# Spread reads moved to SyncE's queue, product and token sums dealt out over wave slots, two batches' attention set at fixed waves

## The chip, the cores and the metric

The kernel runs on one core of a Trainium2 chip. The metric is the device time of one execution in microseconds: 317.69 us is the median of 8 runs before the change (316.64 to 319.45).

A core has five engines with a queue of their own each: TensorE (PE; its weight loads are shown as PEld), VectorE (DVE), ScalarE (ACT), GpSimd (POOL) and SyncE (SP), which here only issues DMAs. Instructions of one engine run in order; between engines they wait on semaphores.

## What is computed

```python
# attention: B, H, S, D = 4, 4, 1088, 32; S1, S2 are 8 x 32
phi(x) = outer(S1 x, S2 x)                 # 64 features per token
kv = sum_s phi(k)_s v_s^T                  # 64 x 32 per head
z  = sum_s phi(k)_s
attn = (phi(q) kv) / (phi(q) z + 1e-6)
# feed-forward: x is attn as (4352 tokens, 128), d_ff = 1536
gate = sigmoid(x @ w_gate)
out  = (gate * (x @ w_val)) @ w_out        # 4352 x 128
```

The arithmetic is in float32. The weights and S1, S2 arrive as 64-bit floats and are narrowed on the chip in the first 50 us.

## The kernel before

The feed-forward runs over 9 chunks of tokens: eight of 512 (numbers 0 to 7) and one of 256. A chunk is done in waves. A wave is one group of 128 columns of d_ff (two groups in the last chunk): `w1` multiplies the chunk's tokens with w_gate and w_val into one of two PSUM tiles `wave`, ACT takes the sigmoid `sg` (L465), and DVE multiplies it with the value part into `g` (L487, `glu`). A chunk of 512 has 12 waves, so chunk c has waves 12c to 12c + 11.

The second product, with w_out, follows some waves later. Chunks 1 to 7 ("fast") do it in pairs of waves with seven products of half size in place of eight. For this each pair needs sums of its activations, `tsum`, made on POOL by `token_sums` (L325: one difference of 128x512, L328, then two ops of 128x256, L334 and L335), and sums of the weights, `ws` (`weight_sums`, L312, L323). `w2_a` (L388) does four of the products into PSUM bank acc0, three slots after the pair's odd wave; `w2_b` (L416) does three into bank acc1, one slot later. After the sixth pair of a chunk, `w2_a` copies half of its bank on ACT (`other`, L401) and adds up on DVE (`res`, L402 and L405), and `w2_b` does the rest (L428 to L432), transposes the result (L436, 64x1024) and issues the stores. The next chunk's first `w2_a` comes two slots after the last one of this chunk.

The order is written out by hand on TensorE, DVE, ACT and POOL; SP's queue is ordered by the build. `slot(group, waves)` (L510) first records a group of attention work, if there is one, and then for each wave: the waiting `glu`, those second products whose slot has come, and the wave's own matmuls. `moe["n"]` counts waves.

Between the waves stands the attention of batches 1 to 3 (L1181 to L1210). For one batch: `turn_k`, `turn_q` transpose K and Q (DVE); `begin` (L1135) projects them on TensorE (`kps`, `cqps`), copies q's projections out (ACT, `cq`) and calls `spread` (L728). `spread` writes `cq` to DRAM (`dq`, on the queue named `put`), and reads it back in broadcast form: two reads of 576 KB into `qp` and four of 288 KB into `bq` (L738, on the queue named `get`), and eight small ones into `a8` and `b8` (L759, on `put`). Before, `put` is SP and `get` is POOL; for the second half of batch 0 they are ACT and SP. Then `outer` makes the features of K (DVE), `sum_z` sums them, `kv_all` multiplies with V (TensorE), `qmult` makes q's features from `qp` and `bq` (DVE), `weights_z`, `ndt` and `parts` (L1156) do the denominators, numerators and the division into `xT`, the input of later chunks. `load_v` and `load_kq` issue the next batch's loads on SP.

Batch 1 has one wave between its steps (`wn` = 1), batches 2 and 3 have two (`wn` = 2), and the steps follow each other from where the last batch ended, so batch 2 begins at wave 28 or 29 and its `parts` stand near wave 41.

Of the kernel before, what the change touches and what calls it, by code (L numbers as in the profile page):

```python
# [16 lines left out]
P = 128  # L17
# [3 lines left out]
def kernel(  # L21
# [282 lines left out]

    xT = const.tile([P, NTOK], F32, tag="xT")

    moe = {"sum": -1, "ci": 0, "w": 0, "n": 0, "ready": 0, "acc": None, "gate": None, "todo": []}

    def fast(ci):
        return 0 < ci < len(tok_chk) - 1 and tok_chk[ci][1] == TCH  # L310
# [11 lines left out]
        ):  # L322
            nc.gpsimd.tensor_tensor(out=out, in0=in0, in1=in1, op=op)  # L323

    def token_sums(g):  # L325
        t = raw.tile([P, 4, HALF], F32, tag="w_in", name="tsum")
        g1 = g[:, 0].rearrange("p (t x) -> p t x", t=2)
        nc.gpsimd.tensor_tensor(  # L328
            out=t[:, :2],
            in0=g.rearrange("p f (t x) -> p t f x", t=2)[:, 1],  # L330
            in1=g1,
            op=ALU.subtract,
        )
        nc.gpsimd.tensor_tensor(out=t[:, 2], in0=t[:, 1], in1=g1[:, 0], op=ALU.add)  # L334
        nc.gpsimd.tensor_tensor(out=t[:, 3], in0=t[:, 2], in1=g[:, 1, :HALF], op=ALU.subtract)  # L335
        return t

    def product(out, lhsT, rhs, start, stop):
        nc.tensor.matmul(  # L339
# [48 lines left out]
    def w2_a(ci, i, g, t):  # L388
        if i == 0:
            moe["sum"] = ci  # L390
            fst["a"] = pso.tile([P, TCH], F32, tag="acc0", name="prod")
        lo, hi = fst["a"][:64], fst["a"][64:]
        w, first, last = w_sb[:, 2], i == 0, i == NJ // 2 - 1
        product(lo[:, :HALF], w[:, 2 * i, :64], g[:, 0, :HALF], first, last)
        product(hi[:, :HALF], w[:, 2 * i + 1, :64], g[:, 1, :HALF], first, last)
        product(lo[:, HALF:], ws[:, 3, i], g[:, 1, HALF:], False, last)
        product(hi[:, HALF:], ws[:, 1, i], t[:, 2], False, last)
        if last:
            e = fst["e"] = raw.tile([P, 2, 2, HALF], F32, tag="w_in", name="other")[:64]
            r = fst["r"] = raw.tile([P, 5, HALF], F32, tag="w_in", name="res")[:64]  # L400
            nc.scalar.copy(out=e[:, 0], in_=hi.rearrange("p (u x) -> p u x", u=2))  # L401
            nc.vector.tensor_tensor(  # L402
                out=ends(r, 1, 3), in0=twice(lo[:, :HALF]), in1=e[:, 0], op=ALU.add
            )
            nc.vector.tensor_tensor(out=r[:, 2], in0=lo[:, HALF:], in1=r[:, 4], op=ALU.add)  # L405

    def twice(x):
        return bass.AP(tensor=x.tensor, offset=x.offset, ap=[list(x.ap[0]), [0, 2], [1, HALF]])
# [7 lines left out]
    def w2_b(ci, i, g, t):  # L416
# [9 lines left out]
        if last:  # L426
            e, r = fst["e"], fst["r"]
            nc.scalar.copy(out=e[:, 1], in_=hi.rearrange("p (u x) -> p u x", u=2))  # L428
            nc.vector.tensor_tensor(out=r[:, 0], in0=lo[:, HALF:], in1=e[:, 1, 1], op=ALU.add)
            nc.vector.tensor_tensor(out=r[:, 4], in0=r[:, 4], in1=r[:, 0], op=ALU.add)  # L430
            nc.vector.tensor_tensor(out=r[:, 3], in0=r[:, 4], in1=e[:, 1, 0], op=ALU.subtract)
            nc.vector.tensor_tensor(  # L432
                out=ends(r, 2, 2), in0=twice(lo[:, :HALF]), in1=ends(r, 2, 2), op=ALU.add
            )
            o_sb = sbA.tile([P, 2, TCH // 32, 32], F32, tag="o_sb", name="o_sb")
            nc.vector.transpose(  # L436
                out=o_sb[:64].rearrange("p d t x -> p (d t x)"),
                in_=r[:, 1:].rearrange("p u x -> p (u x)"),
            )
            store(ci, lambda g4: o_sb[32 * (g4 % 2) : 32 * (g4 % 2) + 32, g4 // 2])  # L440

    def w1():

# [41 lines left out]
        def glu():  # L485
# [3 lines left out]
            if not fast(ci):  # L489
                lag = 3 if ci else 2  # L490
                part = (ci, j0, jn, g.rearrange("p (j t) -> p j t", j=jn))
                todo.append((n + lag, lambda: w2(*part)))
            elif odd:
                part = (ci, j0 // 2, pair, token_sums(pair))
                todo.append((n + 3, lambda: w2_a(*part)))
                todo.append((n + 4, lambda: w2_b(*part)))

# [12 lines left out]
    def slot(group, waves):  # L510
# [4 lines left out]
        for _ in range(waves):  # L515
            more = moe["ci"] < len(tok_chk)
            if more and sum(tok_chk[moe["ci"]]) > moe["ready"]:
                break
            glu()
            while todo and todo[0][0] <= moe["n"]:  # L520
                todo.pop(0)[1]()
            if more:
# [612 lines left out]
    def begin(b):  # L1135
        glu()
        kps(b)
        cq[b] = qcomp(b, (0, 1), (psm, "wave"))
        spread(b, (0, 1), cq[b], nc.sync, nc.gpsimd)

    def q01():
        spread(0, (1,), qcomp(0, (1,), (ps2, "two")), nc.scalar, nc.sync)
# [24 lines left out]
    def kv_all(b):  # L1167
        kv(b, ZS[b])
        kvd(b)
# [8 lines left out]
    slot(lambda: part01(lambda: narrow_w(NJ - 1, 3)), 1)  # L1178
    slot(last01, 1)
    v_t[1] = load_v(1)  # L1180
    for b in range(1, B):  # L1181
        more = b + 1 < B
        wn = 1 if b == 1 else 2
        turn_k(b)
        if b > 1:
            turn_q(b, 0)
        slot(None, wn)
        if b == 1:
            turn_q(b, 0)
        turn_q(b, 1)  # L1190
        slot(lambda: begin(b), 1)
        for pi in range(2):
            outer(b, pi)
            slot(None, wn)
        for step in range(2):
            sum_z(b, step)
            slot(None, wn)
            if b == 1 and step == 0:
                masks()
        slot(lambda: kv_all(b), wn)  # L1200
        if more:
            v_t[b + 1] = load_v(b + 1)
        qmult(b, 0)
        weights_z(b)
        slot(lambda: ndt(b), 1)
        qmult(b, 1)
        load_kq(b + 1)
        if b == 1:
            slot(None, 1)
        slot(lambda: parts(b), wn + 5)  # L1210
    slot(None, 10**3)


# [28 lines left out]
```

## Time and profile before

| | |
|---|---|
| median of 8 runs | 317.69 us |
| the profiled execution | 316.64 us, span on the core 314.8 us |
| TensorE, DVE, POOL, ACT busy | 294.7, 184.3, 160.2, 88.9 us |
| `g` (DVE L487) | x102, mean 683 ns |
| token sums on POOL (L328, L334, L335) | x42 each, mean 1376, 729, 816 ns |
| spread reads on POOL (L738) | x18, mean 590 ns to issue; 8.2 us (`qp`) and 9.9 us (`bq`) median to landing |
| granted TensorE clock, mean | 0.989 |

The span goes from the first instruction to the last. A line of a timeline gives the start in us from the start of the span, the duration, the engine, the source line, what is written and read, the shape, and in brackets how long the engine had been idle before it and what ended that. The end of a wave's matmuls is best seen from the start of its sigmoid, 0.04 to 0.1 us later.

### The profile page before, as it was taken

What the parts mean: (1) busy time and instruction counts of PE and PEld (TensorE: products, weight loads), DVE (VectorE), ACT (ScalarE), POOL (GpSimd) and SP (SyncE); (2) the same over time, 40 slices, a digit from 0 to 9 for tenths busy, and PEclk for the clock granted to TensorE, in tenths of its full rate; (3) what the DMA queues carried; (4) which work ended last, traced back from release to release, by engine and by line L of the source; (5) the groups of instructions that cost most, each with busy time, mean ns of one, the idle gap of its engine ahead of it and who ended that gap; (6) DMA issues with size and microseconds to landing.
All of it is one profiled execution on the core that took longest, in us unless ns stands there. A gap on an engine that the chain in (4) does not pass through costs nothing.

```text
span 314.8 us, 5511 instructions
## 1 busy us (share of the span) xinstructions
PE 294.7 (94%) x2176; PEld 152.6 (48%) x2176; DVE 184.3 (59%) x310; ACT 88.9 (28%) x164; POOL 160.2 (51%) x196
## 2 busy tenths in 40 slices
PE   8899999489999779988999999899999999999995
PEld 3444432135455344543564455443556465546853
DVE  6997798807737735388247853894327323722461
ACT  3566523102123212330224221222223222322320
POOL 1556560964363495515657874436463654566300
PEclk9999999959999999999999999999999999999999
DMA  7994241872400387126001880002000200010021
GB/s 221 354 315 111 66 143 52 188 172 77 144 0 0 73 186 157 31 47 173 3 0 49 192 171 3 2 1 35 1 0 2 33 0 2 7 29 0 0 35 17
DMA packets 30553, 24.35 MB, mean 77 GB/s; under 512 B 20480, under 2 KB 25728, under 8 KB 30528
## 3 DMA queue, kind: packets, MB, share of 16 engines
q1 hardware_dynamic: 27024, 16.15, 19.3%
q0 software_dynamic: 2592, 7.08, 9.9%
q10 hardware_dynamic: 912, 0.77, 0.9%
q8 instruction: 17, 0.28, 0.4%
q14 instruction: 8, 0.07, 0.1%
HBM read 20.73 MB, written 3.26 MB: 76 GB/s over the span
## 4 chain that ended last, share of the span: by engine, by line
PE 62%; DVE 12%; POOL 10%; DMA 8%; issue 5%; ACT 1%; SPq 1%; POOLq 0%; DVEq 0%
PE wave L457 40%; PE prod L339 17%; POOL head L118 3%; DMA v<-in_v_dram 3%; POOL tsum L328 2%; DMA w_in<-in_moe_w_out_dram 2%; PE moeout L370 2%; POOL ws L323 2%; DVE g L487 2%; DMA w_in<-in_moe_w_gate_dram 1%; DVE o_sb L436 1%; POOL bq L738 1%; DVE head L109 1%; DVE w_sb L127 1%; PE kvz L788 1%
## 5 line engine op out<-in xcount | busy, mean ns | idle before, releaser
L457 PE MATMUL wave<-xT,w_sb 128*64 128x512 f32 (+3 forms) x820 | 213.6, 572 | 0.8 <-DVE g L487 0.8
L487 DVE TENSOR_TENSOR g<-wave,sg 128x512 f32<-128x512 f32 x102 | 69.6, 683 | 110.0 <-ACT sg L465 105.7
L457 PEld LDWEIGHTS wave<-xT,w_sb 128*64 128x64 f32 (+1 forms) x820 | 82.5, 141 | 69.4 <-issue 50.6
L465 ACT ACTIVATE sg<-wave 128x512 f32<-128x512 f32 x102 | 61.0, 598 | 193.4 <-PE wave L457 186.1
L328 POOL TENSOR_TENSOR tsum<-g 128x512 f32<-128x512 f32 x42 | 57.8, 1376 | 95.5 <-DVE g L487 95.5
L339 PE MATMUL prod<-tsum,ws 128*64 128x256 f32 x252 | 68.0, 387 | 7.4 <-POOL tsum L334 7.4
L339 PEld LDWEIGHTS prod<-tsum,ws 128*64 128x64 f32 x252 | 33.2, 139 | 21.7 <-POOL tsum L334 8.8
L335 POOL TENSOR_TENSOR tsum<-tsum,g 128x256 f32<-128x256 f32 x42 | 34.3, 816 | 3.3
L339 PE MATMUL prod<-g,w_sb 128*64 128x256 f32 x168 | 34.0, 382 | 0.1
L334 POOL TENSOR_TENSOR tsum<-tsum,g 128x256 f32<-128x256 f32 x42 | 30.6, 729 | 3.3
L339 PE MATMUL prod<-tsum,w_sb 128*64 128x256 f32 x84 | 25.6, 388 | 0.0
L339 PE MATMUL prod<-g,ws 128*64 128x256 f32 x84 | 25.0, 379 | 0.0
L339 PEld LDWEIGHTS prod<-g,w_sb 128*64 128x64 f32 x168 | 15.9, 137 | 18.1 <-issue 16.8
L118 POOL TENSOR_TENSOR head<-head,tail 128x384 int32<-128x384 int32 (+2 forms) x14 | 13.3, 952 | 18.2 <-DVE head L109 15.1
L370 PE MATMUL moeout<-g,w_sb 128*128 128x512 f32 (+1 forms) x48 | 18.9, 503 | 0.3 <-DVE w_sb L127 0.3
L339 PEld LDWEIGHTS prod<-tsum,w_sb 128*64 128x64 f32 x84 | 11.3, 139 | 7.9 <-issue 6.9
L339 PEld LDWEIGHTS prod<-g,ws 128*64 128x64 f32 x84 | 11.5, 137 | 3.3
L370 PEld LDWEIGHTS moeout<-g,w_sb 128*128 128x128 f32 x48 | 8.5, 189 | 8.3 <-issue 4.2
L646 DVE TENSOR_TENSOR kp<-kab 128x1152 f32<-128x1152 f32 (+2 forms) x10 | 10.6, 1081 | 0.0
L766 DVE TENSOR_TENSOR qp<-qp,bq 128x1152 f32<-128x1152 f32 (+1 forms) x7 | 9.1, 1296 | 0.0
L738 POOL DMA_DIRECT2D qp<-dq x6 | 3.6, 595 | 10.3 <-DMA dq<-cq 10.3
L436 DVE STREAM_TRANSPOSE o_sb<-res 64x1024 f32<-64x1024 f32 x7 | 8.7, 1236 | 0.2
(114 smaller groups left out, 196.1 us busy)
## 6 DMA issues: line engine op xcount, KB each, us to landing
qp<-dq POOLq DMA_DIRECT2D x6, 576.0 KB, 8.2
bq<-dq POOLq DMA_DIRECT2D x12, 288.0 KB, 9.9
v<-in_v_dram SPq DMA_DIRECT2D x16, 144.0 KB, 4.2
kq<-in_k_dram SPq DMA_DIRECT2D x3, 544.0 KB, 3.8
kq<-in_q_dram SPq DMA_DIRECT2D x3, 544.0 KB, 4.7
w_in<-in_moe_w_out_dram SPq DMA_DIRECT2D x6, 256.0 KB, 7.2
w_in<-in_moe_w_gate_dram SPq DMA_DIRECT2D x5, 256.0 KB, 5.5
w_in<-in_moe_w_val_dram SPq DMA_DIRECT2D x5, 256.0 KB, 6.7
```

Of the source, the lines that this page charges most:

```text
L118: nc.gpsimd.tensor_tensor(out=head, in0=head, in1=tail, op=ALU.add)
L328: nc.gpsimd.tensor_tensor(out=t[:, :2], in0=g.rearrange("p f (t x) -> p t f x", t=2)[:, 1], in1=g1, op=ALU.subtract,)
L334: nc.gpsimd.tensor_tensor(out=t[:, 2], in0=t[:, 1], in1=g1[:, 0], op=ALU.add)
L335: nc.gpsimd.tensor_tensor(out=t[:, 3], in0=t[:, 2], in1=g[:, 1, :HALF], op=ALU.subtract)
L339: nc.tensor.matmul(out=out, lhsT=lhsT, rhs=rhs, start=start, stop=stop, skip_group_check=True)
L370: nc.tensor.matmul(out=moe["acc"][:, :tw], lhsT=w_sb[:, 2, j, :], rhs=g[:, jj, :tw], start=(j == 0), stop=(j == NJ - 1),)
L436: nc.vector.transpose(out=o_sb[:64].rearrange("p d t x -> p (d t x)"), in_=r[:, 1:].rearrange("p u x -> p (u x)"),)
L457: nc.tensor.matmul(out=wv[d, which, jj * tw + o : jj * tw + o + tp], lhsT=w_sb[:, which, j0 + jj, d], rhs=xT[:, t0 + o : t0 + o + tp], sta ...
L465: nc.scalar.activation(out=sg, in_=wv[:, 0], func=ACTF.Sigmoid)
L487: nc.vector.tensor_tensor(out=g, in0=wv[:, 1], in1=sg, op=MUL)
L646: eng.tensor_tensor(out=KP[b][:, pi, j0:j1].rearrange("p j m (i l) -> p (j m) i l", i=R), in0=bass.AP(tensor=a0.tensor, offset=a0.offset, ...
L766: nc.vector.tensor_tensor(out=q0, in0=q0, in1=half(BQ[b], n), op=MUL)
```

## The change

Four things are edited.

1. In `begin`, the spread reads (`get`) go on SP's queue instead of POOL's.
2. `token_sums` makes its four sums as four POOL ops of 128x256 instead of one of 128x512 and two of 128x256: the first after the even wave's `g`, three after the odd wave's.
3. The sums of a chunk's products become small functions in a list `moe["late"]`, of which `slot` runs one per wave, after `glu`. Only the first (and the two ACT copies) stays in `w2_a` and `w2_b`. The transpose becomes two of 64x512. The stores come with the second one.
4. Batches 2 and 3 no longer follow with two waves between steps: each step is recorded when the wave count has reached a number of a table. Batch 1 keeps its order, written out.

```diff
-    def token_sums(g):
-        t = raw.tile([P, 4, HALF], F32, tag="w_in", name="tsum")
-        g1 = g[:, 0].rearrange("p (t x) -> p t x", t=2)
-        nc.gpsimd.tensor_tensor(
-            out=t[:, :2],
-            in0=g.rearrange("p f (t x) -> p t f x", t=2)[:, 1],
-            in1=g1,
-            op=ALU.subtract,
-        )
-        nc.gpsimd.tensor_tensor(out=t[:, 2], in0=t[:, 1], in1=g1[:, 0], op=ALU.add)
-        nc.gpsimd.tensor_tensor(out=t[:, 3], in0=t[:, 2], in1=g[:, 1, :HALF], op=ALU.subtract)
-        return t
+    def token_sums(g, t, odd):
+        def sub(u, in0, in1):
+            nc.gpsimd.tensor_tensor(out=t[:, u], in0=in0, in1=in1, op=ALU.subtract)
+
+        if not odd:
+            sub(0, g[:, 0, HALF:], g[:, 0, :HALF])
+            return
+        sub(2, g[:, 1, HALF:], t[:, 0])
+        sub(3, t[:, 2], g[:, 1, :HALF])
+        sub(1, g[:, 1, HALF:], g[:, 0, HALF:])
...
             nc.scalar.copy(out=e[:, 0], in_=hi.rearrange("p (u x) -> p u x", u=2))
-            nc.vector.tensor_tensor(
-                out=ends(r, 1, 3), in0=twice(lo[:, :HALF]), in1=e[:, 0], op=ALU.add
-            )
-            nc.vector.tensor_tensor(out=r[:, 2], in0=lo[:, HALF:], in1=r[:, 4], op=ALU.add)
+
+            add(ends(r, 1, 3), twice(lo[:, :HALF]), e[:, 0])
+            moe["late"] += [lambda: add(r[:, 2], lo[:, HALF:], r[:, 4])]
+
+    def add(out, in0, in1, op=ALU.add):
+        nc.vector.tensor_tensor(out=out, in0=in0, in1=in1, op=op)
...
             nc.scalar.copy(out=e[:, 1], in_=hi.rearrange("p (u x) -> p u x", u=2))
-            nc.vector.tensor_tensor(out=r[:, 0], in0=lo[:, HALF:], in1=e[:, 1, 1], op=ALU.add)
-            nc.vector.tensor_tensor(out=r[:, 4], in0=r[:, 4], in1=r[:, 0], op=ALU.add)
-            nc.vector.tensor_tensor(out=r[:, 3], in0=r[:, 4], in1=e[:, 1, 0], op=ALU.subtract)
-            nc.vector.tensor_tensor(
-                out=ends(r, 2, 2), in0=twice(lo[:, :HALF]), in1=ends(r, 2, 2), op=ALU.add
-            )
             o_sb = sbA.tile([P, 2, TCH // 32, 32], F32, tag="o_sb", name="o_sb")
-            nc.vector.transpose(
-                out=o_sb[:64].rearrange("p d t x -> p (d t x)"),
-                in_=r[:, 1:].rearrange("p u x -> p (u x)"),
-            )
-            store(ci, lambda g4: o_sb[32 * (g4 % 2) : 32 * (g4 % 2) + 32, g4 // 2])
+
+            def fifth_seventh():
+                add(ends(r, 2, 3), twice(lo[:, :HALF]), ends(r, 2, 2))
+                add(r[:, 0], lo[:, HALF:], e[:, 1, 1])
+
+            def last_sums():
+                add(r[:, 3], r[:, 4], e[:, 1, 0], op=ALU.subtract)
+                add(r[:, 3:5], ends(r, 3, 2), twice(r[:, 0]))
+
+            def turned(d):
+                nc.vector.transpose(
+                    out=o_sb[:64, d].rearrange("p t x -> p (t x)"),
+                    in_=r[:, 1 + 2 * d : 3 + 2 * d].rearrange("p u x -> p (u x)"),
+                )
+
+            def turn_store():
+                turned(1)
+                store(ci, lambda g4: o_sb[32 * (g4 % 2) : 32 * (g4 % 2) + 32, g4 // 2])
+
+            moe["late"] += [fifth_seventh, last_sums, lambda: turned(0), turn_store]
...
-            elif odd:
-                part = (ci, j0 // 2, pair, token_sums(pair))
+                return
+            if not odd:
+                moe["t"] = raw.tile([P, 4, HALF], F32, tag="w_in", name="tsum")
+            token_sums(pair, moe["t"], odd)
+            if odd:
+                part = (ci, j0 // 2, pair, moe["t"])
...
             glu()
+            if moe["late"]:
+                moe["late"].pop(0)()
             while todo and todo[0][0] <= moe["n"]:
...
-        spread(b, (0, 1), cq[b], nc.sync, nc.gpsimd)
+        spread(b, (0, 1), cq[b], nc.sync, nc.sync)
...
+    def until(n):
+        slot(None, n - moe["n"])
+
+    plan = {2: (27, 29, 30, 31, 32, 34, 36, 37, 38, 39, 42, 44)}
+    plan[3] = (48, 49, 51, 53, 56, 57, 58, 59, 60, 61, 63, 68)
+    for b in range(2, B):
+        at = iter(plan[b])
+        until(next(at))
         turn_k(b)
-        if b > 1:
-            turn_q(b, 0)
...
+        for n in range(2):
+            until(next(at))
+            turn_q(b, n)
+        until(next(at))
         slot(lambda: begin(b), 1)
         for pi in range(2):
+            until(next(at))
             outer(b, pi)
-            slot(None, wn)
         for step in range(2):
+            until(next(at))
             sum_z(b, step)
-            slot(None, wn)
...
-        slot(lambda: kv_all(b), wn)
-        if more:
+        until(next(at))
+        slot(lambda: kv_all(b), 1)
+        if b + 1 < B:
             v_t[b + 1] = load_v(b + 1)
+        until(next(at))
         qmult(b, 0)
+        slot(lambda: ndt(b), 1)
         weights_z(b)
-        slot(lambda: ndt(b), 1)
+        until(next(at))
         qmult(b, 1)
         load_kq(b + 1)
...
-        slot(lambda: parts(b), wn + 5)
+        until(next(at))
+        slot(lambda: parts(b), 1)
     slot(None, 10**3)
```

In the built order, each chunk's late sums stand as follows, if s is the slot of its last `w2_a`: the sum r[2] in slot s + 1 (before the last `w2_b`), `fifth_seventh` in s + 2, `last_sums` in s + 3, the first transpose in s + 4, the second and the stores in s + 5. Chunk 7 has s = 98, and the last wave is 101.

## The prediction

> **What bounds the kernel now.** I read the page first, then the waits, then the timeline engine by engine around the waits that end on TensorE. From the page:
>
> ```profile
> span 314.8 us, 5511 instructions
> PE 294.7 (94%) x2176; PEld 152.6 (48%) x2176; DVE 184.3 (59%) x310; ACT 88.9 (28%) x164; POOL 160.2 (51%) x196
> PEclk9999999959999999999999999999999999999999
> PE 62%; DVE 12%; POOL 10%; DMA 8%; issue 5%; ACT 1%; SPq 1%; POOLq 0%; DVEq 0%
> ```
>
> TensorE is the bound: no other engine passes 59%. What can be won is the time in which it has nothing, or runs at half clock (the 5 in the ninth slice, near 63 to 70 us). The timeline of TensorE, 40 to 130 us:
>
> ```profile
> 64.04 0.69 PE L339 MATMUL prod<-tsum,ws 128*64 128x256 f32 x1 [5.32 <-POOL tsum L334]
> 64.95 3.62 PE L457 MATMUL wave<-xT,w_sb 128*64 128x512 f32 x7
> ...
> 105.28 0.72 PE L713 MATMUL cqps<-qT,skq 64*32 64x288 f32 x16 [1.69 <-DVE qT L547]
> ...
> 115.99 0.43 PE L339 MATMUL prod<-tsum,ws 128*64 128x256 f32 x1 [1.68 <-POOL tsum L334]
> ```
>
> It waits 5.32 us for a token sum of POOL; the wave after that takes 3.6 us instead of about 1.9. Why POOL is late stands in its own timeline, 44 to 65 us:
>
> ```profile
> 46.43 0.59 POOL L323 TENSOR_TENSOR ws<-w_sb 128x192 f32<-128x192 f32 x1
> 55.28 0.76 POOL L738 DMA_DIRECT2D qp<-dq  x1 [8.26 <-DMA dq<-cq]
> ...
> 58.72 0.68 POOL L323 TENSOR_TENSOR ws<-w_sb 128x192 f32<-128x192 f32 x1
> ...
> 61.75 1.44 POOL L328 TENSOR_TENSOR tsum<-g 128x512 f32<-128x512 f32 x1
> 63.27 0.72 POOL L334 TENSOR_TENSOR tsum<-tsum,g 128x256 f32<-128x256 f32 x1
> ```
>
> POOL stood 8.26 us in front of the first spread read of batch 1 until q's features had landed in DRAM, issued six reads (3.5 us), and only then made the weight sums and token sums queued behind. Around batch 2 the Vector engine is late (its timeline, 95 to 106 us):
>
> ```profile
> 98.19 1.29 DVE L536 STREAM_TRANSPOSE kT<-kq 128x1088 f32<-128x1088 f32 x1
> ...
> 102.64 1.24 DVE L436 STREAM_TRANSPOSE o_sb<-res 64x1024 f32<-64x1024 f32 x1
> 103.81 0.64 DVE L487 TENSOR_TENSOR g<-wave,sg 128x512 f32<-128x512 f32 x1
> 104.38 0.75 DVE L547 STREAM_TRANSPOSE qT<-kq 128x576 f32<-128x576 f32 x1
> ```
>
> From 97.1 us it has no gap: chunk 1's sums, K's and q's transposes stand in one heap, and cqps waits for the last one. The starts of the sigmoid (ACT L465) are the beat of the waves:
>
> ```profile
> 57.92 0.60 ACT L465 ACTIVATE sg<-wave 128x512 f32<-128x512 f32 x1 [1.12 <-PE wave L457]
> ...
> 71.25 0.60 ACT L465 ACTIVATE sg<-wave 128x512 f32<-128x512 f32 x1 [2.03 <-PE wave L457]
> ...
> 219.32 0.60 ACT L465 ACTIVATE sg<-wave 128x512 f32<-128x512 f32 x1 [1.99 <-PE wave L457]
> ...
> 229.26 0.60 ACT L465 ACTIVATE sg<-wave 128x512 f32<-128x512 f32 x1 [2.00 <-PE wave L457]
> ```
>
> Four quiet slots (waves 66 to 70) take 9.94 us, so 2.485 each; from wave 65 (216.73) to 98 (298.67) it is 81.94/33 = 2.483. The last 98 us are at TensorE's own pace; nothing is to be won there.
>
> **What the Trainium skill says.** "TensorE: Matmul & The Clock Gate", Part 1: after an idle window of about 3.4 us the array's clock is halved until it has been busy as long. The trace agrees: 5.32 us idle, then a granted clock of 0.50 from 64.0 to 69.4 us. "SBUF — State Buffer", section on the two separate sides: a Vector op with both inputs in SBUF and a GpSimd op that reads SBUF exclude each other for a whole instruction. It agrees: POOL's L335 at 180.32 took 1.80 us instead of 0.72 beside the Vector engine's L822. "DMA: Bandwidth & Descriptors", "Issuing engines are not separate DMA queues": changing the issuer saves only the issuer's time. The b = 0 reads, already on SP, land like POOL's (4.9 us for qp, against 5.3 to 6.4 for the first of each POOL batch).
>
> **The change part by part.** Losses first, each a stretch between sigmoid starts less the same stretch undisturbed.
> - Waves 15 to 17, 13.33 us less 4.97: 8.36 (5.32 idle, and 5.4 us at half clock costs 2.7).
> - Waves 28 to 29, 5.77 less 3.87 (the same step of batch 3, 49 to 50): 1.90.
> - Waves 29 to 33, 11.79 less 9.94: 1.85.
> - Waves 37 to 41 (kv, ndt, parts of batch 2), 17.20 less 14.47 (waves 17 to 21, the same for batch 1): 2.73.
> - Waves 50 to 54, 11.38 less 9.94: 1.44. Waves 58 to 62, 15.20 less 14.47: 0.73. Waves 62 to 65, 8.87 less 7.46: 1.41.
>
> Sum 18.42 us. All stretches between keep the beat.
>
> Reads to SP: 6 issues of 0.6 us and the wait leave POOL for each of three batches. POOL then meets wave 12's g at 51.7: one difference 0.7, four weight sums 2.6, wave 13's g at 55.8, and t[2] stands near 56.6; the product that waited until 64.0 can run at 58.3. The first loss and those after 29 and 50 lose their cause. What SP queues behind: the reads wait there for dq as POOL did (SP's a/b reads already stood at 55.0), issue until about 59, and the eight a/b reads follow. In the built order the last six of these each wait for the landing of the DMA eight places before, a spread read. Spread traffic took from 56.7 to 69.6 us; SP's b = 0 half took about the same per byte, so qp/bq land near 63 and 70, the last b8 near 72. With the stall gone waves 16 to 20 end near 60.4, 62.8, 66.9, 69.8, 72.4. qmult(1,0) comes after wave 17's g at 64.2, so it is free; qmult(1,1) after 69.2 waits up to 1 us, covered because g has about 3.2 us from its wave's end until the wave after next needs its bank, and takes 1.4; denj at 72.4 is a tie: 0 to 1 us, I take 0.3.
>
> Token sums: 1.38 + 0.73 + 0.82 = 2.9 us in one burst become one 0.7 after the even g and three (2.2 to 2.3) after the odd one. TensorE's first need, t[2], is ready 0.75 us after the odd g instead of 2.1. No cost: POOL stays near 3.0 of 4.97 us a pair.
>
> Product sums: 0.68 + 4 x 0.42 + 0.68 + 1.24 = 4.3 us of the Vector engine in two slots become 0.68, 0.42, 1.1, 1.1, 0.65, 0.65 in six. A slot leaves it 2.485 - 0.68 = 1.8 us, so each fits. What is late next is the bank: the last read of acc1 (fifth_seventh) ends about 0.64 + 0.69 + 1.1 + small gaps = 2.5 us after its wave's end, the next product into that bank comes after 0.86 + 1.72 = 2.58. A tie, at seven chunk ends; from 0 to 0.7 each, if a POOL op is in the way. I take 0.5 in all.
>
> Fixed waves: batch 2 begins at wave 31 instead of 28, parts at 44 and 68. Per slot the attention adds at most 1.3 (kT), 0.75 (qT), 0.95 (kab), 1.35 (outer), 2.3 (second step of sum_z), 1.2 or 1.4 (qmult); the worst sums in one slot (turn_k with the sum r[2], 1.7; last_sums with qmult, 2.5 at wave 42) pass 1.8 by less than g's spare 1.8. parts has no chunk sums beside it (these end at slots 43 and 67), as in batch 1, where it cost nothing. Reads have from wave 31 to 39 and 53 to 61, 20 us for about 16 (stores that stand before dq on SP included). So I count the other five losses as gone.
>
> End: chunk 7's two transposes now stand behind the last g (before: 302.1), and its four stores on SP in front of the final pair. They issue from about 311.0 for 1.8 us, where the final pair went at 311.5 and 311.9 with 1.7 us to land: +1.3 us.
>
> Sum: 314.8 - 18.4 + 0.3 + 0.5 + 1.3 = 298.5. Around the span lie 316.64 - 314.8 = 1.84, giving 300.3; the profiled execution was the fastest of eight, 1.05 under the median 317.69. Forecast 301.3, own range 299.5 to 303.5.
>
> **The rivals.**
> - Vector stalls only move. The heaps are dealt out but the work stays (59% busy), and lock waits of up to 0.7 us come on each two-input op. Then only POOL's losses go, 8.36 + 1.85 + 1.44 = 11.65: 316.64 - 11.65 + 2.1 + 1.05 = 308.1. Against it: the slots worked out above.
> - The bank: if each of seven chunk ends costs 0.65 more, 4.5 us: 305.8. For it the tie; against it that waves 75 and 87 now show a delayed g and no loss.
> - Slower: SP serves the reads late. dq, stores, six reads and eight short ones now go in one line. If a batch's reads took twice as long, 29 us from dq's landing, qmult(1,0) would hold g from 67.4 (64.2 + 3.2) to near 84, TensorE would stand 16 us and then run at half clock (3 us), and batches 2 and 3 would lose about 10 each: 301.3 + 39 = 340. It decides only above some 13 us for the first half; SP's own b = 0 reads needed under 8 from issue.
> - The change doesn't do what it says: the built order has each step at its wave, so hardly.
>
> **How the numbers follow.** Forecast 0.72, moved stalls 0.13, bank 0.10, slower 0.04, nothing 0.01. So faster by over 0.3% (1 us, what this kernel's runs can tell) 0.95, within 0.01, slower 0.04. The range goes from 298.5, below nearly all of the forecast's, to 306.5, which takes in the bank and leaves out the rest of moved stalls and the slow case, under 2 in 10.
>
> **What would show it.** No POOL issue of reads; the PEclk row without a 5; wave 17's sigmoid near 62.9; no wait of TensorE above 0.5 us after 58; 4 slots per 9.94 us past wave 20 but for kps/cqps, kv and parts; the last store issued some 1.3 us after the last transpose. A wait of cqps, nps or a wave for DVE over 1 us would speak for the first rival, of prod for DVE res at slots 28, 29, 40, 41 and so on for the second, of DVE qp for a DMA for the third.

## The result and the profile after

The changed kernel takes 300.58 us (median of 11 runs, 299.95 to 303.55), the kernel before 317.69 us (32 runs); the ratio is 0.947, its 95% interval 0.945 to 0.949. The forecast was 301.3. The profiled execution's span is 298.9 us, and the working had come to 298.5.

The page of the changed kernel, with the rows that answer to those shown of before:

```profile
span 298.9 us, 5583 instructions
PE 290.0 (97%) x2176; PEld 152.5 (51%) x2176; DVE 187.5 (63%) x317; ACT 88.9 (30%) x164; POOL 160.9 (54%) x220
PEclk9999999999999999999999999999999999999999
PE 77%; DMA 13%; DVE 4%; POOL 2%; SPq 2%; issue 1%; ACT 1%; POOLq 0%; DVEq 0%
```

TensorE's busy time fell by under 5 us (294.7 to 290.0; matmuls at half clock are part of that), the rest of the 15.9 us was its idle time: its busy share of the span rose from 94 to 97%, its share of the chain that ended last from 62 to 77%. VectorE and GpSimd fell from 12 and 10% of that chain to 4 and 2% without having less to do: 187.5 us and 160.9 us are no less than before. DMA rose from 8 to 13%: between 52 and 73 us the chain now goes through batch 1's write of `dq` and the reads of it on SP. The 5 in the clock row is gone.

The waits of TensorE in the changed kernel (what waits, for what; us in total, times, longest), the two of them that lie after 20 us:

```profile
PE moeout L368 <- DVE res L405: 1.4, 1, 1.4
...
PE denj L932 <- DMA b<-dq: 0.3, 1, 0.3
```

The wait for token sums, 7.4 us in three pieces before, does not occur, nor do those for qT and qp. What is left is one wait of 1.4 us that the prediction did not have, and one of 0.3 for a late read. The same in the beat of the waves (timeline of ScalarE; first column the start):

```profile
57.82 0.60 ACT L474 ACTIVATE sg<-wave 128x512 f32<-128x512 f32 x1 [1.12 <-PE wave L466]
60.40 0.60 ACT L474 ACTIVATE sg<-wave 128x512 f32<-128x512 f32 x1 [1.97 <-PE wave L466]
62.97 0.60 ACT L474 ACTIVATE sg<-wave 128x512 f32<-128x512 f32 x1 [1.97 <-PE wave L466]
...
280.86 0.60 ACT L474 ACTIVATE sg<-wave 128x512 f32<-128x512 f32 x1 [1.12 <-PE wave L466]
```

These are waves 15, 16, 17 and 98. From 15 to 17 it takes 5.15 us where it took 13.34, and from 15 to 98 223.04 where it took 240.75: 17.71 us gained. The last stretches give some back: from 98 to 101 the wave starts take 10.76 instead of 9.61, and from wave 101 to the end it is 7.32 instead of 6.55. The start is 0.1 shorter. -17.71 + 1.15 + 0.77 - 0.1 = -15.9, which is the difference of the spans, 314.8 - 298.9.

The heap that VectorE had around the start of batch 2 is spread out. In its timeline the sums (`res`), the transposes of K and q and the halves of `o_sb` now stand in different slots, each with a `g` between them, and TensorE's `cqps` (last line, from TensorE's timeline) no longer waits for `qT`:

```profile
90.42 1.29 DVE L551 STREAM_TRANSPOSE kT<-kq 128x1088 f32<-128x1088 f32 x1
91.65 0.65 DVE L496 TENSOR_TENSOR g<-wave,sg 128x512 f32<-128x512 f32 x1
...
98.46 0.76 DVE L562 STREAM_TRANSPOSE qT<-kq 128x576 f32<-128x576 f32 x1
99.15 0.64 DVE L496 TENSOR_TENSOR g<-wave,sg 128x512 f32<-128x512 f32 x1
99.73 0.68 DVE L440 STREAM_TRANSPOSE o_sb<-res 64x512 f32<-64x512 f32 x1
...
101.25 0.69 PE L728 MATMUL cqps<-qT,skq 64*32 64x288 f32 x16
```

### The profile page after: what moved, and what is told of

It is laid out like the page before. It is cut to its first block, busy times and chain, and to the rows that moved or that the text cites. A ratio compares the mean times of both kernels' runs of the same rounds, so it can differ in the third digit from the quotient of the medians.

```text
span 298.9 us, 5583 instructions
## 1 busy us (share of the span) xinstructions
PE 290.0 (97%) x2176; PEld 152.5 (51%) x2176; DVE 187.5 (63%) x317; ACT 88.9 (30%) x164; POOL 160.9 (54%) x220
## 4 chain that ended last, share of the span: by engine, by line
PE 77%; DMA 13%; DVE 4%; POOL 2%; SPq 2%; issue 1%; ACT 1%; POOLq 0%; DVEq 0%
PE wave L466 49%; PE prod L337 20%; DMA bq<-dq 5%; PE moeout L368 3%; DMA w_in<-in_moe_w_out_dram 2%; POOL head L118 2%; DMA kq<-in_q_dram 2%; DMA w_in<-in_moe_w_val_dram 2%; PE nps L997 1%; DMA v<-in_v_dram 1%; DVE w_sb L127 1%; SPq L753 1%; DVE head L109 1%; PE kvz L803 1%; DMA dq<-cq 1%
## 5 line engine op out<-in xcount | busy, mean ns | idle before, releaser
L466 PE MATMUL wave<-xT,w_sb 128*64 128x512 f32 (+3 forms) x820 | 211.1, 566 | 0.0
L466 PEld LDWEIGHTS wave<-xT,w_sb 128*64 128x64 f32 (+1 forms) x820 | 84.2, 140 | 65.7 <-issue 49.4
L327 POOL TENSOR_TENSOR tsum<-g 128x256 f32<-128x256 f32 x84 | 66.8, 798 | 24.6 <-DVE g L496 24.4
L327 POOL TENSOR_TENSOR tsum<-g,tsum 128x256 f32<-128x256 f32 x42 | 34.2, 814 | 65.3 <-DVE g L496 65.1
L337 PE MATMUL prod<-tsum,ws 128*64 128x256 f32 x252 | 62.3, 381 | 0.0
L337 PEld LDWEIGHTS prod<-tsum,ws 128*64 128x64 f32 x252 | 30.9, 136 | 16.7 <-issue 12.6
L327 POOL TENSOR_TENSOR tsum<-tsum,g 128x256 f32<-128x256 f32 x42 | 33.6, 800 | 3.3
L337 PE MATMUL prod<-g,w_sb 128*64 128x256 f32 x168 | 34.8, 382 | 0.0
L337 PEld LDWEIGHTS prod<-g,w_sb 128*64 128x64 f32 x168 | 15.9, 136 | 19.1 <-issue 15.7
L440 DVE STREAM_TRANSPOSE o_sb<-res 64x512 f32<-64x512 f32 x14 | 9.6, 688 | 0.0
L405 DVE TENSOR_TENSOR res<-prod,other 64x512 f32<-64x512 f32 (+1 forms) x14 | 7.6, 544 | 3.1 <-ACT other L399 3.1
```

What stands on the lines that cost most here:

```text
L327: nc.gpsimd.tensor_tensor(out=t[:, u], in0=in0, in1=in1, op=ALU.subtract)
L337: nc.tensor.matmul(out=out, lhsT=lhsT, rhs=rhs, start=start, stop=stop, skip_group_check=True)
L405: nc.vector.tensor_tensor(out=out, in0=in0, in1=in1, op=op)
L440: nc.vector.transpose(out=o_sb[:64, d].rearrange("p t x -> p (t x)"), in_=r[:, 1 + 2 * d : 3 + 2 * d].rearrange("p u x -> p (u x)"),)
L466: nc.tensor.matmul(out=wv[d, which, jj * tw + o : jj * tw + o + tp], lhsT=w_sb[:, which, j0 + jj, d], rhs=xT[:, t0 + o : t0 + o + tp], sta ...
```

## The experiments

The runs stand in groups; those of one group ran beside the same runs of the kernel before. All stretches below are differences of sigmoid starts in one profiled execution each, in us (the last digit can be off by one from the rounded starts); the first two columns are the two kernels of the change. The kernel before was slower beside some groups than beside others, so medians of different groups are compared by their ratios to it; its own median is in the last row.

| waves | before | changed | reads on SP only | reads back | old order | sums at once | token sums back | best (chunk 7 at once, batch 1 later) |
|---|---|---|---|---|---|---|---|---|
| 15-17 | 13.34 | 5.14 | 6.56 | 10.95 | 5.14 | 5.14 | 6.56 | 5.14 |
| 20-22 | 7.42 | 8.39 | 7.42 | 7.42 | 11.20 | 9.20 | 7.42 | 7.46 |
| 22-28 | 14.67 | 14.67 | 14.67 | 14.67 | 17.07 | 14.67 | 14.67 | 15.06 |
| 28-68 | 121.48 | 110.60 | 120.96 | 113.03 | 111.10 | 112.55 | 111.98 | 110.60 |
| 98-101 | 9.61 | 10.76 | 9.62 | 10.76 | 10.76 | 9.59 | 10.76 | 9.30 |
| 101-end | 6.55 | 7.32 | 6.35 | 7.38 | 7.33 | 6.36 | 7.33 | 6.36 |
| span | 314.8 | 298.9 | 307.0 | 306.4 | 304.6 | 300.1 | 301.1 | 296.2 |
| median | 317.69 | 300.58 | 308.92 | 308.42 | 305.55 | 301.43 | 302.72 | 297.66 |
| kernel before, same group | 317.69 | 317.69 | 319.06 | 319.06 | 319.06 | 319.06 | 317.96 | 317.96 |

### The reads alone

```
-        spread(b, (0, 1), cq[b], nc.sync, nc.gpsimd)
+        spread(b, (0, 1), cq[b], nc.sync, nc.sync)
```

> The kernel before with one part of the change alone: all reads of the spread buffer issued on SP. Theory (each part removes its own losses): of the 18.4 us of loss in the table of waves, waves 15 to 17 (8.36), 29 to 33 (1.85) and 50 to 54 (1.44) belong to reads on POOL, so about 11.6 us go, less the costs of batch 1's later landings (about 1): span 303 to 305, and no half clock. Rival (the order of the attention and of the sums is what matters, the reads' queue is secondary): the stalls of waves 15 to 17 only change hands, span 311 or more. If a/b reads on SP land later than need in batch 1, a wait of about 1 us appears in waves 19 to 21.

Measured: 308.92 us, ratio 0.969 (0.965 to 0.974), span 307.0. Profile against profile that is 7.8 us gained where the theory had some 11 and the rival under 4: it lies between. By the medians of the group (319.06 for the kernel before, of three runs) it is 10.1, because all three of those runs were slower than the profiled one. The theory's span of 303 to 305 was missed either way, and so was its "no half clock". Waves 15 to 17 give 6.78 us of the 8.36, waves 29 to 33 1.91 as expected, waves 50 to 54 nothing (11.37 before and here). The rest of the first stretch is still a token sum, in the timeline of TensorE of this run:

```profile
59.59 0.43 PE L339 MATMUL prod<-tsum,ws 128*64 128x256 f32 x1 [1.19 <-POOL tsum L334]
```

And 1.42 us were lost in waves 37 to 41, where the change touches nothing: the clock fell there (see the last section).

### The reads put back on POOL in the changed kernel

The same line, the other way round.

> The changed kernel with one part undone: 12 of the spread reads of batches 1 to 3 go back to POOL's queue. Theory: POOL issues reads ahead of wave 14's pair's ws and token sums again, TensorE waits over 4 us near 58 to 65 us and runs at half clock after it: 7 to 9 us back there, 0 to 1.5 in each of batches 2 and 3, less the 1 us of batch 1's late landings; span 305.5 to 309.5. Rival (the token sums split in two, with one operation ahead of the odd half, or the fixed waves, already took the stall away): span within 2 of the changed kernel's 298.9.

Measured: 308.42 us, 0.968 (0.963 to 0.972), span 306.4, 7.5 longer than the changed kernel's: the theory's range, and not the rival's. (The reads that went back are 18, six in each of three batches; the 12 of the expectation is a slip.) Waves 15 to 17 lose 5.81 again, less than the 7 to 9 that were expected there, 33 to 37 1.43, 54 to 58 0.85; batch 1's waves 20 to 22 win 0.97 back. GpSimd's timeline in this run:

```profile
51.88 0.73 POOL L327 TENSOR_TENSOR tsum<-g 128x256 f32<-128x256 f32 x1 [4.80 <-DVE g L496]
54.82 0.76 POOL L753 DMA_DIRECT2D qp<-dq  x1 [2.21 <-DMA dq<-cq]
...
57.17 1.15 POOL L753 DMA_DIRECT2D bq<-dq  x2
58.26 1.08 POOL L323 TENSOR_TENSOR ws<-w_sb 128x192 f32<-128x192 f32 x1
...
61.72 0.90 POOL L327 TENSOR_TENSOR tsum<-g,tsum 128x256 f32<-128x256 f32 x1
```

The even half's difference runs at 51.88, ahead of the reads, and then all else stands behind them until 58.3, as in the kernel before; TensorE waits 3.88 us where it waited 5.32 in the kernel before (the theory had over 4). In the changed kernel nothing stands between:

```profile
51.71 0.73 POOL L327 TENSOR_TENSOR tsum<-g 128x256 f32<-128x256 f32 x1 [4.79 <-DVE g L496]
52.40 0.59 POOL L323 TENSOR_TENSOR ws<-w_sb 128x192 f32<-128x192 f32 x1
53.07 0.59 POOL L323 TENSOR_TENSOR ws<-ws,w_sb 128x192 f32<-128x192 f32 x1
53.74 1.59 POOL L323 TENSOR_TENSOR ws<-w_sb,ws 128x192 f32<-128x192 f32 x1
...
55.84 1.85 POOL L327 TENSOR_TENSOR tsum<-g,tsum 128x256 f32<-128x256 f32 x1
```

### The old order of batches 2 and 3

```
-    plan = {2: (27, 29, 30, 31, 32, 34, 36, 37, 38, 39, 42, 44)}
-    plan[3] = (48, 49, 51, 53, 56, 57, 58, 59, 60, 61, 63, 68)
+    wn = 2
     for b in range(2, B):
...
-            until(next(at))
-            outer(b, pi)
+            outer(b, pi)
+            slot(None, wn)
```

> The changed kernel with the attention of batches 2 and 3 in its old order of two waves a step, the sums still dealt out and the reads on SP. Theory: some of the stalls behind VectorE in waves 28 to 33, 37 to 41 and 54 to 65 come back, since heaps of attention meet the dealt sums: 2 to 5 us, span 301 to 304. Rival (the dealt sums alone had taken these stalls away, fixed waves only move work): within 1 us of 298.9. Second rival (dealt sums need the fixed waves, else a bank is held): 305 or more, with the wait of TensorE at product sums behind ScalarE or VectorE.

Of the six slots that stood between batch 1's last step and batch 2 in the kernel before only one is left in it, so batch 2 begins five waves earlier: K's and q's feature matmuls of batch 2 come after wave 23 and not after wave 28. Measured: 305.55 us, 0.959 (0.951 to 0.966), span 304.6, 0.6 above the theory's range. Waves 28 to 68, which it was about, take only 0.5 us more, but some 1.3 us of batch 2's matmuls have moved out of that stretch; over waves 22 to 68, which hold batches 2 and 3 in both kernels, it is 2.9 (128.17 against 125.28). The largest loss is in waves 20 to 25 (5.2 us, of which these moved matmuls are 1.3), where batch 1's own reads were late in this execution (timeline of TensorE):

```profile
73.88 0.49 PE L932 MATMUL denj<-b,zw 64*64 64x160 f32 x4 [1.38 <-DMA b<-dq]
74.67 0.49 PE L932 MATMUL denj<-b,zw 64*64 64x160 f32 x4 [0.31 <-DMA b<-dq]
```

and half clock came after it, from 76.0 to 79.4 us. The program up to that point is the changed kernel's own. So this run could not tell what it was made for; it was repeated below without the late reads.

### The product sums at once

```
-            moe["late"] += [lambda: add(r[:, 2], lo[:, HALF:], r[:, 4])]
+            add(r[:, 2], lo[:, HALF:], r[:, 4])
...
-            moe["late"] += [fifth_seventh, last_sums, lambda: turned(0), turn_store]
+            fifth_seventh()
+            last_sums()
+            turned(0)
+            turn_store()
```

> The changed kernel with the product sums of a chunk run where its products end, as before, instead of dealt out over later slots; reads on SP and fixed waves stay. Theory: VectorE has five to six sums and two transposes in a row at each of eight chunk ends, so g of the next wave is late where attention sits in the same slots: 1.5 to 4 us in waves 28 to 65, less the 0.5 us of the bank tie, the 1.1 us before chunk 8 and up to 0.8 at the tail: span 298 to 301. Rival (the dealt sums are what the schedule rests on): 303 or more. Rival (they are worth nothing, the fixed waves do it all): 296 to 297.5.

Measured: 301.43 us, 0.946 (0.940 to 0.952), span 300.1: the theory. Waves 28 to 68 lose 1.95, with g late for two waves (0.43 and 0.50 us of TensorE's time, after 131 and 197 us); chunk 8 and the tail win back 1.17 + 0.96, a late read of batch 1 costs 0.8, and in this execution the waves start 0.7 later. So, in this version of the kernel, dealing out wins 1.95 us beside the attention and gives 2.13 back at the end: by the time alone this part of the change is worth next to nothing.

### The changed kernel again

> The changed kernel itself, beside the next three on the same chip: median 300.3 to 301.5 us, profiled span 298.5 to 300. A second profile also tells how much of the wait in batch 1 (waves 20 to 22 took 8.39 us against 7.42 before) changes from run to run: the two kernels profiled since, whose program is the same up to there, took 9.20 and 11.20.

Measured: 300.28 us, 0.945 (0.943 to 0.947), span 298.5. In this execution waves 20 to 22 take 7.42 us and no wait for b is left. So batch 1's loss comes and goes with the landing of its reads: 8.39, 7.42, 9.20, 11.20, and 7.60 in the run after the next, all with the same program up to there. SP's last read of batch 1 was issued at 71.76, 70.32, 73.35, 72.95 and 71.14 us. Counted from the sigmoid of wave 15 that is 13.9, 12.1, 14.8, 15.2 and 13.2 us: the later the read, the larger the loss.

### The token sums in one burst

```
-            token_sums(pair, moe["t"], odd)
             if odd:
-                part = (ci, j0 // 2, pair, moe["t"])
+                part = (ci, j0 // 2, pair, token_sums(pair))
```

> The changed kernel with the token sums as before: three GpSimd operations after the odd half's g (the first 128x512) instead of one after the even half's g and three short ones after the odd's. The prediction counted the split at nothing of its own: span within 0.5 of the changed kernel. Rival, from the run with the reads alone, where TensorE still waited 1.19 us for a token sum at 59.6: the split is what takes that rest away, so waves 15 to 17 take 6.5 us instead of 5.14 and the span is 1.2 to 1.6 us longer.

Measured: 302.72 us, 0.953 (0.951 to 0.955), against 300.28 of the changed kernel in the same group: 2.4 us, more than the rival had. Waves 15 to 17 take 6.56, as with the reads alone, so the 1.42 us left over there are this burst, and the prediction's "no cost" for the change of the token sums was in truth a gain that it left out; and waves 28 to 68 lose another 1.38 in pieces of 0.1 to 0.5. GpSimd's timeline:

```profile
55.96 2.32 POOL L328 TENSOR_TENSOR tsum<-g 128x512 f32<-128x512 f32 x1 [6.42 <-DVE g L498]
58.36 1.58 POOL L334 TENSOR_TENSOR tsum<-tsum,g 128x256 f32<-128x256 f32 x1
60.02 0.73 POOL L335 TENSOR_TENSOR tsum<-tsum,g 128x256 f32<-128x256 f32 x1
```

It stood idle for 6.42 us before the burst, and the second operation of the burst, whose result the product needs, ended at 59.9. In the changed kernel this sum, t[2], was ready at 57.7, because its first operand had been made at 51.7.

### The last fast chunk at once

```
-            moe["late"] += [fifth_seventh, last_sums, lambda: turned(0), turn_store]
+            rest = [fifth_seventh, last_sums, lambda: turned(0), turn_store]
+            if ci == len(tok_chk) - 2:
+                for f in rest:
+                    f()
+            else:
+                moe["late"] += rest
```

and the same for r[2] in w2_a.

> The changed kernel with the sums of the last fast chunk alone (chunk 7) run where its products end; chunks 0 to 6 stay dealt out. Theory: the wait of 1.42 us before chunk 8's first moeout goes (waves 98 to 101 take 9.6 us instead of 10.76), the tail from wave 101's sigmoid to the end gives back up to 0.77: span 1.1 to 1.9 us shorter than the changed kernel's. Rival: with the sums in a heap, g of wave 99 or 100 comes late and the same time is lost there: within 0.4.

Measured: 298.77 us, 0.940 (0.938 to 0.943), 1.5 under the changed kernel's 300.28; span 295.8. Waves 98 to 101 take 9.30 instead of 10.76, and the tail 6.34 instead of 7.32. The theory's mechanism holds, and nothing is lost in their place. By the median the gain lies in its range of 1.1 to 1.9; the profiled execution, the fastest of the six, gained 2.7 against the second profile of the changed kernel, since both stretches gave more than expected (1.46 and 1.06). What the changed kernel does there, in its timelines of TensorE and of VectorE:

```profile
280.64 0.65 PE L337 MATMUL prod<-tsum,ws 128*64 128x256 f32 x4
282.72 1.10 PE L368 MATMUL moeout<-g,w_sb 128*128 128x256 f32 x4 [1.42 <-DVE res L405]
```

```profile
281.56 0.69 DVE L496 TENSOR_TENSOR g<-wave,sg 128x512 f32<-128x512 f32 x1 [1.10 <-ACT sg L474]
282.17 0.40 DVE L405 TENSOR_TENSOR res<-prod,res 64x256 f32<-64x256 f32 x1
```

The sum r[2] waits for its turn behind g of wave 98, although chunk 8's first product needs its bank in the same slot. The same place in this run goes on without a gap:

```profile
279.97 0.65 PE L337 MATMUL prod<-tsum,ws 128*64 128x256 f32 x4
280.55 1.13 PE L368 MATMUL moeout<-g,w_sb 128*128 128x256 f32 x4
```

### Batch 1 a wave later as well

```
-    slot(lambda: ndt(1), 1)
+    slot(lambda: ndt(1), 2)
     qmult(1, 1)
```

> As the run before (chunk 7's sums at once), and the second half of batch 1's products with bq, and what follows it, one wave later. Theory: the reads that SP issues late have landed by then, VectorE no longer stands 3 us in front of g of wave 19, waves 20 to 22 take 7.4 and no wait for b is left: 1 us shorter than the run before, in all 2 to 3 us shorter than the changed kernel, span 296 to 297. Rival: the later attention of batch 1 meets the dealt sums of chunk 1 or the start of batch 2 at wave 27, and a stall of the same size stands there: no shorter than the run before.

Measured: 297.66 us, 0.937 (0.935 to 0.939), 2.6 us under the changed kernel in the same group; the intervals of the two ratios do not meet. Span 296.2. Against the run before it, whose only difference is this wave, it is 1.1. Its six runs lie between 297.25 and 297.95; in the same group the run before went from 297.60 to 299.22 and the changed kernel from 299.68 to 300.71, and in the group of the result from 299.95 to 303.55. SP's last read of batch 1 went out at 73.6 us in this profile, 15.6 after wave 15 and later than in any of the five above, and the list of TensorE's waits has none above 0.15 us from 20 us to the end. A rest of the loss is still there, in TensorE's weight loads:

```profile
74.89 0.19 PEld L941 LDWEIGHTS denj<-b,zw 64*64 64x64 f32 x4 [0.81 <-DMA b<-dq]
```

Waves 20 to 22 take 7.46 us here and 7.05 in all four runs below, so about 0.4 us of this profile are that read. This version beats both kernels.

### Order and sums, taken apart without the late reads

The last four are made from the version above: the old order (with its earlier start of batch 2), all sums at once, the sums of chunks 5 to 7 at once (`if ci >= 5`), and the old order with all sums at once. They ran in a group of their own, in which the kernel before has 318.72 us. The version above was not run again beside them; the run with chunks 5 to 7 at once, whose median is nearly the same, stands for it there.

> The run with chunk 7's sums at once and batch 1 a wave later, and in it the attention of batches 2 and 3 in its old order (a repeat of the earlier run with the old order, where late reads of batch 1 came into it). Theory: with batch 1's reads out of the way the old order costs little as long as the sums are dealt out; the stretches from wave 28 to 68 were 0.5 us longer in the earlier run: 0.5 to 1.5 us longer than the run it is made from, span 296.7 to 297.8. Rival (the fixed waves themselves are worth the losses named in the prediction for waves 28 to 41 and 54 to 65): 4 us or more longer.

> The same base with the product sums of every fast chunk at once and the attention of batches 2 and 3 at its fixed waves. Theory, from the waves of the earlier run with sums at once: 1.9 us more in waves 28 to 68, 0.2 less after: 1.5 to 2 us longer than the base, span 297.7 to 298.3. Rival (dealt sums worth nothing once the attention has its fixed waves): within 0.5.

> The base with the sums of chunks 5, 6 and 7 at once, whose ends (waves 77, 89, 98) have no attention beside them; chunks 1 to 4 stay dealt out. Theory: the bank ties at 77 and 89 go, 0.1 to 0.3 us shorter than the base, which three or five rounds may not tell from nothing; no stall comes in its place.

> The same base with both undone: all sums at once and the attention of batches 2 and 3 in the old order; reads on SP, the split token sums and the later batch 1 stay. Theory (one hides what the other takes away: each alone, undone, costs 0.5 to 2 us): together they cost what the kernel before and the run with the reads alone lose in waves 28 to 68, 9 to 10.5 us: span 305 to 307. Rival (the two add up): 2 to 4 us longer than the base, span 298 to 300.

| | median us | ratio to before (95%) | span | waves 22-68 |
|---|---|---|---|---|
| version above | 297.66 | 0.937 (0.935-0.939) | 296.2 | 125.7 |
| old order | 299.32 | 0.939 (0.935-0.944) | 297.9 | 127.4 |
| sums at once | 299.65 | 0.940 (0.936-0.945) | 298.1 | 127.3 |
| both | 301.45 | 0.945 (0.940-0.950) | 300.3 | 130.4 |
| chunks 5 to 7 at once | 297.57 | 0.934 (0.930-0.937) | 295.9 | 125.7 |

By the medians the old order costs 1.7 us, 0.1 beyond the expected end by its span, and not the rival's 4. The sums at once cost 2.0, as expected. The ratios' intervals of these two overlap that of the version above, but within their own group no run of theirs is below 299.0 and none with chunks 5 to 7 at once is above 297.82. The expectation for both, 9 to 10.5 us, fell: they cost 3.8 us, about the sum of the two, the rival's figure (its span, 300.3, is 0.3 above the rival's range). Chunks 5 to 7 at once can't be told from chunk 7 alone (0.09 us are won at waves 77 and at 89, 0.29 given back before wave 101).

The fallen one says most. "Both" has the sums in heaps and the steps of two waves, like the kernel before. To compare it with the run with the reads alone, a stretch is needed that holds the same work in both, and since batch 2 has moved this is waves 20 to 68. With the reads alone moved they took 143.05 us, in "both" they take 137.42, and in the changed kernel without a late read (its second profile) 132.71. Between the first two of these runs lie the split token sums, worth 1.4 in waves 28 to 68 of the changed kernel (the run with the burst), batch 1's later half, the sums' new grouping, and that batches 2 and 3 stand some four waves earlier. In the kernel before, batch 2's first matmuls came after wave 28 and its last products after wave 40, each on top of the sums of a chunk; in "both" they come after waves 24 and 36. TensorE's waits for g are then 1.41, 0.93 and 0.47 us. The two largest, and what VectorE did before the first of them (timelines):

```profile
84.58 1.94 PE L475 MATMUL wave<-xT,w_sb 128*64 128x512 f32 x8 [1.41 <-DVE g L505]
99.47 1.94 PE L475 MATMUL wave<-xT,w_sb 128*64 128x512 f32 x8 [0.93 <-DVE g L505]
```

```profile
83.24 0.71 DVE L571 STREAM_TRANSPOSE qT<-kq 128x512 f32<-128x512 f32 x1 [1.14 <-DMA kq<-in_q_dram]
```

The first is not the sums' doing: VectorE stood in front of g, waiting for q's load to land. It makes waves 22 to 28 1.26 us longer than in the run with the old order alone, and without it the costs of the two in waves 22 to 68 nearly add up: 1.7 and 1.6 alone, 3.4 together.

Of the 10.3 us between the reads alone and the changed kernel, "both" has 5.6. Less the 1.4 of the token sums that is some 4.2 of 9.0: a little under half of what fixed waves and dealt sums seemed to win came without them. How much exactly is open, since the half clock cost the run with the reads alone 1.4 us, and the late load cost "both" 1.3. That it is the shift of the old steps off the chunk ends is argued from these runs: the kernel before with nothing but a shift was not run.

## Why the prediction was right, and where its terms were off

- **Losses gone, 18.42 less 0.3 and 0.5 for ties: 17.6.** Measured 17.71 from wave 15 to wave 98. Wave 17's sigmoid was put near 62.9 and came at 62.97. The three ways of losing (a token sum behind reads, a clock that falls after it, heaps on VectorE) are what the profile shows gone.
- **"Reads to SP" took all of 8.36 + 1.85 + 1.44.** The total is right and the split is not. Of the 8.36, putting the reads back returns 5.81 and moving them alone takes 6.78; 1.42 is the token sums' burst, which the prediction described (t[2] ready 0.75 us after the odd g instead of 2.1) and counted at "no cost" and no gain. Measured, the split is worth 2.4 us. The 1.44 of waves 50 to 54 is not the reads' at all: moving them left 11.37 us as it was. Waves 44 to 54 together became 1.4 shorter with the rest of the change (27.63 to 26.26).
- **The losses left to the sums and the steps: 1.90 + 2.73 + 0.73 + 1.41 = 6.77 (four losses; the prediction's "five" is a miscount).** They are gone in the changed kernel, but the runs do not give the whole to these two parts: undone together, in the kernel with batch 1 a wave later, they cost 3.8 us, and part of the rest may be the mere place of batches 2 and 3.
- **POOL's operations.** t[2] was put at 56.6 and came at 57.7: one weight sum took 1.59 us instead of 0.59 and two token sums 1.85 and 1.65 instead of 0.7 to 0.8. VectorE ran operations with two inputs in SBUF at the time (`kp` at 53.15 and 55.62, `z` at 57.62). This is what the Trainium skill, "SBUF — State Buffer", section on the two separate sides, states of the pair; the product's matmuls ran from 58.0 without a gap, so it cost nothing.
- **Batch 1's tie, 0 to 1 us, 0.3 taken.** The mechanism was right and the size too small. Measured 0.97 in this profile and 0 in the next; in kernels with the same program up to there, up to 3.8 with the half clock that follows. The term rested on SP's b = 0 reads landing "about the same per byte" as POOL's. They did not with all reads of a batch on one queue (last section). One step one wave later takes the loss down to 0.4 us in one profile and to nothing in four.
- **Bank ties, 0.5 in all.** Measured 0.1 at each of waves 29, 41, 65, 77 and 89 (2.59 to 2.61 us for a wave instead of 2.5): right.
- **The tail, +1.3.** Measured 0.77, and 0.98 against the run with chunk 7 at once. SP issues the six last stores from 293.58 on in 2.99 us, chunk 7's four in front of the final pair, as predicted; the size was too large.
- **Missed: 1.15 us before chunk 8.** The bank was only examined for the next fast chunk, whose first product comes two slots on. Chunk 8 is not a fast one: its moeout runs earlier and into the bank that r[2] still had to read. Undone, it gave 1.46 us back.
- **The rivals.** Moved stalls did not appear (in TensorE's timeline no wait for DVE above 0.15 us from 20 to 280 us). The bank as a rival (0.65 at each chunk end) appeared once, in a place not named. SP's late reads are real but cost 1 us, not 39: the first half landed 0.8 us after VectorE wanted it, which hid behind the waves.

The span's nearness owes something to errors that cancel: 298.5, less 0.1 for the losses, 0.5 for the tail and 0.1 for the start, plus the missed 1.15, is 298.9. The 0.7 too little for batch 1 is inside the first of these, made good by losses that were 0.8 larger than counted. And the forecast's surcharge of 1.05, for a profiled execution that had been the fastest of eight, wasn't needed: 298.9 and the 1.84 around a span make 300.7, and the median is 300.58.

## What to carry to other kernels

When work on one engine falls in heaps at fixed points (here sums at every twelfth wave), first ask where the other heaps lie relative to these points: here the old steps, standing four waves earlier, had a little under half of what dealing both heaps out won, though a shift alone was not run. When work is dealt out late, look at every consumer of the buffer it holds, and above all at the last, irregular one: the steady state hid the wait before chunk 8. A step whose inputs come by DMA needs its margin in the worst landing of several executions, not in one: one wave of slack took away 1.1 us of the median, and the range of six runs went from 1.6 to 0.7 us.

## What the runs showed of the hardware

**The same waits, with and without a fall of the clock.** Moving the reads alone shifted the stall of waves 37 to 41 by 9 us and left its two waits, of 1.3 and 1.2 us, the same, yet TensorE went to half clock after it and lost 1.42 us. The Trainium skill, "TensorE: Matmul & The Clock Gate", Part 1, says that activity is judged in windows of 3413 ns that run freely and aren't started by the work. The traces agree with that step: the clock is halved from 134.06 to 137.48 us in the run with the reads alone (one step) and from 62.58 to 69.41 in the kernel before (two), and full from there to 315.17 (72 steps). Laid out in these steps, the stall looks different in the two runs (stretch; us; busy time and instructions of each engine, granted clock, DMA share, GB/s). First the kernel before, then the run with the reads alone:

```profile
137.67:141.09 3.42, 2.41 (x14) 0.87 (x10) 3.32 (x6) 1.00 (x3) 0.00 (x0) 1.00 0.03 5
141.09:144.50 3.41, 1.92 (x41) 0.87 (x48) 3.16 (x6) 0.00 (x0) 2.47 (x2) 1.00 0.29 43
```

```profile
130.65:134.06 3.41, 1.00 (x10) 0.35 (x8) 3.34 (x7) 0.60 (x1) 1.14 (x1) 1.00 0.26 41
134.06:137.48 3.42, 3.32 (x42) 0.95 (x44) 2.29 (x8) 0.00 (x0) 2.63 (x3) 0.50 0.44 73
```

In the first the edge of a window falls into the stall, and TensorE works 2.41 and 1.92 us of the two windows; in the second nearly the whole stall lies in one, with 1.00 us of work. So the phase of the stall is the likely cause, and the 1.42 us are then chance rather than an effect of the reads. The page speaks of an idle window; here one with 1.00 us of work in it was enough. How much work keeps the clock does not come out: 1.72 us (103.54 to 106.95, the kernel before) kept it, and 1.82 us (72.60 to 76.01, the run with the old order) did not.

**The reads moved more slowly on one queue than on two.** Batch 1's traffic in the changed kernel (all reads on SP) and, in the second fence, in the run with the six large reads back on POOL:

```profile
57.00:61.00 4.00, 4.00 (x27) 1.85 (x25) 3.97 (x8) 1.20 (x2) 3.92 (x4) 1.00 0.92 199
61.00:65.00 4.00, 4.00 (x95) 2.15 (x93) 2.65 (x4) 0.97 (x2) 3.77 (x10) 1.00 0.76 150
65.00:69.00 4.00, 4.00 (x31) 1.85 (x29) 3.46 (x5) 0.75 (x2) 3.16 (x4) 1.00 0.55 154
```

```profile
57.00:61.00 4.00, 1.79 (x12) 0.60 (x8) 3.97 (x8) 0.60 (x1) 3.84 (x7) 1.00 1.04 235
61.00:65.00 4.00, 2.33 (x9) 0.99 (x11) 1.00 (x2) 0.00 (x0) 3.84 (x7) 0.82 1.05 231
65.00:69.00 4.00, 4.00 (x29) 1.61 (x29) 0.69 (x1) 0.67 (x2) 3.24 (x8) 0.75 0.78 163
```

The last column is GB/s: 150 to 199 on one queue, 231 and 235 on two for as long as there is enough to move. The Trainium skill, "DMA: Bandwidth & Descriptors", "Issuing engines are not separate DMA queues", has it that a second issuer saves only the time to issue; here more differed. The other engines' work isn't the same in the two stretches, the short reads went out at other times, and the two queues cut the large reads differently (2592 packets on POOL's, listed as software_dynamic, 1728 more on SP's, hardware_dynamic, for the same 7.08 MB). So that the number of queues is the cause is not settled.

The short reads went out late because SP held 16 of the 24 for the landing of a read before it. In the waits of SP's queue in the changed kernel:

```profile
SPq L774 <- DMA bq<-dq: 24.9, 12, 3.7
SPq L774 <- DMA qp<-dq: 6.1, 4, 2.2
```

That is 31 us over three batches. The prediction had these waits in the built order; how much later the landings behind them would come is what it had too small.
